# Linear attention and a gated MLP on one core: two tile transposes moved to DMA, and a 1024x1024 product made in four bursts of sixteen small products

## The chip, the core and the metric

One core of a Trainium2 chip runs the whole program as one launch. The time is device microseconds for one execution of the kernel. Comparisons are made between medians of several runs of each kernel on the same chip. One execution was also recorded by the hardware profiler; all rows below are from that execution.

## What is computed

```python
x  = A_x                                   # 1 x 2048 x 1024, bf16
xn = layernorm(x)
q, k, v = split(xn @ wqkv)                 # 32 heads of 32
pq, pk = phi(q), phi(k)                    # phi(t) = (t+1 if t>0 else exp(t)) + 1e-6
kv  = einsum("bhsd,bhse->bhde", pk, v)     # per head, 32 x 32
z   = einsum("bhsd->bhd", pk)
o   = (pq @ kv) / (pq @ z + 1e-6)
s   = o @ wo
g   = silu((silu(xn @ w_gate) * (xn @ w_up)) @ w_down)    # inner width 3584
out = x + s * g
```

The change touches two intermediate things. The first is the transposed form of xn for two of its sixteen tiles of 128 rows. The second is M, a 1024 x 1024 matrix: for each head, the transposed 32 x 32 matrix kv/z times that head's 32 rows of wo. With M, the attention half of the output is one product of the scaled pq with M.

## The kernel before, in words

**A planner writes the order.** The code first lists operations (`Plan.op`), each with an engine, the regions that it reads and writes, and an assumed cost. `Plan.schedule` then orders all engines with a list scheduler. A DMA is taken to occupy SyncE for 0.47 or 1.22 us and to land some microseconds later. Due times are counted back from the TensorE work that needs the result; for a DMA the due time moves forward by a larger allowance than for an on-chip operation. TensorE operations keep the listed order, except that within a window of six (`WINDOW=6`) the first that is ready may go ahead. The emitted program is fixed: each engine executes its list in order and waits on semaphores. One change to one operation can therefore shift the order of others. All 128-row matmul groups are recorded at line 309, all transposes on TensorE at 316, all ScalarE copies and activations at 441, all VectorE two-operand operations at 452, all plain DMA issues on SyncE at 455.

**The opening (to about 24 us).** x arrives in tiles of 128 rows. `ln_tile(i)` takes statistics on VectorE (772 to 779), a power on GpSimd (782), and normalises, on VectorE for tiles 0 and 1 and on ScalarE for the others, into one of two slots (`xn_ring`). `t_tile(i)` makes the transposed tile. For tiles 0 to `NPE-1` = 3 it uses TensorE: eight transposes of 128x128 into PSUM and a copy to SBUF; tile 2 and tile 3 each have one 128x1024 copy on ScalarE (line 821). For tiles 4 to 15 it uses one DMA transpose issued by SyncE (line 808). A slot of `xn_ring` can be filled again once its transpose has read it. Tiles 0 and 1 are multiplied by the k and v weights directly (`p_piece`, 64 matmuls of 512 columns).

**The k and v stage (to about 118 us).** Tiles 2 to 15 go in pairs u through a seven-product scheme for a 2 by 2 block product (`Set.step(m)`, m = 1 to 7, four matmuls each). Product 1 and product 2 read only the first tile of the pair; product 5 reads the sum of blocks of both tiles, made on VectorE by `x_sums(u)`. After product 1 its bank is copied on ScalarE to a second bank (`put1`), after product 5 its bank is copied to SBUF (`put5`). `a_tile(i)` adds one tile's pk^T v into three PSUM banks with eight matmuls of 129 columns. It depends only on the k and v of its own tile, and the calls stand in a queue named `fill`, from which the loop takes one after each product 6.

**M.** When kv is complete, VectorE scales and masks it and TensorE transposes it (`kvt`). `m_build(g, c)` then makes one 128 x 512 block of M from one 128x128 stationary tile (four heads on its diagonal, zeros elsewhere) and 512 columns of wo. It takes one PSUM bank, ScalarE copies the bank to a staging slot in SBUF (`mst_ring`), and SyncE stores it in DRAM. There are sixteen blocks. They are hung on steps of three column pairs of the next stage ("g 0", "u 0", "q 1") through the table `at` at lines 1696 and 1697. M is read back later by `s_load`.

**Column pairs and banks.** From `q 0` on, the work goes in pairs of sets, with a half-sized version of products 1 and 5 (`Joint`, steps nj1a to nj5d). The listed order of a pair, woven into the rest of the previous one, is

```python
LINK = "7_0 nj1a 3_0 7_1 nj1b nj5a 3_1 nj1c nj5b 4_0 nj1d nj5c 4_1 n2_0 nj5d n6_0 n2_1 n6_1".split()
```

where n marks the new pair, "6_1" is product 6 of set 1, and each plain step is four matmuls. PSUM has eight banks, dealt out in the order in which they come free in the list (`balloc`, `bfree`). A set holds two banks from product 1 on and a third, in place of the first, from product 6 on; a Joint takes two banks at its first part.

**The remainder.** The gate, up, q and s pairs and the down product follow for two halves of the rows, and take from 118 us to the end.

Of the kernel before, what the change touches and what calls it, by code (L numbers as in the profile page):

```python
# [9 lines left out]
ACT = mybir.ActivationFunctionType  # L10
# [3 lines left out]
FP16 = mybir.dt.float16  # L14
KB = 1024
# [301 lines left out]
    return last  # L317


def build_kernel(nc, A_x, A_wqkv, A_wo, B_w_gate, B_w_up, B_w_down, out, WINDOW=6, NWARM=15, NPE=4, LEAD=12.0):  # L320
    S, D, FF = 2048, 1024, 3584
    NT, KT, NG, NPAIR = 16, 8, 8, 14
    EPS_LN, EPS_PHI = 1e-5, 1e-6
# [9 lines left out]
    with ExitStack() as es:  # L333
# [20 lines left out]
        def named(*key):  # L354
            return Region([key])

        H = Arena("H", 84 * KB)
# [19 lines left out]
        m_scr = nc.dram_tensor("m_scratch", [D, D], FP16)  # L377
        m_v = m_scr.rearrange("(g p) c -> p g c", p=128)
# [13 lines left out]
        def balloc(fresh=False):  # L392

            if fresh and bare and (len(banks) < 3 or freed[bare[0]] < freed[banks[0]]):
                b = bare.popleft()
                is_bare.discard(b)
                return b
            return banks.popleft()
# [7 lines left out]
        def bfree(b):  # L406
            freed[b] = len(PL.ops)
            (bare if b in is_bare else banks).append(b)
# [7 lines left out]
        def dsem(name):  # L416
            if name not in semn:
                semn[name] = sem("d_" + name)
            return semn[name]
# [8 lines left out]
        def pe_mm(reads, writes, mms):  # L428
            return PL.op("pe", reads, writes, partial(_mm_group, mms), mm_cost(mms))
# [10 lines left out]
        def act(reads, writes, o, i, func, src="ps", **kw):  # L440
            q = PL.op("act", reads, writes, lambda h: h.activation(o, i, func, **kw),  # L441
                      nel(o) / (1000.0 if "bias" in kw or not isinstance(kw.get("scale", 1.0), float) else 1200.0)
                      + (0.055 if src == "ps" else 0.095))
            if func != ACT.Identity:
                PL.table(q, func)
            return q
# [7 lines left out]
        def dma(reads, writes, o, i, s, nbytes, cow=None, after=None):  # L454
            return PL.op("sp", reads, writes, lambda h: h.dma_start(o, i), 0.47, sem=s,  # L455
                         nbytes=nbytes * (1.45 if nbytes in (128 * KB, 896 * KB) else 1.0), cow=cow,
                         after=after)
# [114 lines left out]
        for n in range(NWARM):  # L572
            b = n % 8
# [318 lines left out]
        def a_tile(i):  # L892
            q = i % 4
            pk = pkv[i].ap()
            mms = [(kv_ap(g), pk[:, g * 128:(g + 1) * 128], vext[q][:, g, 0:129], i == 0 and g % 3 == 0, i == NT - 1)
                   for g in range(NG)]
            pe_mm([pkv[i].r, named("vx", q, 0), named("vx", q, 1), named("vx1", q), vx_r[q]], [bank_r[b] for b in kvb], mms)
# [76 lines left out]
        p_piece(1, 1, 0)  # L974
        for b in tb:
            bfree(b)
        fill = deque([partial(a_tile, 0), partial(a_tile, 1)])
        stats_of = {1: x_sums(1)}
        todo = [(u, w) for u in range(1, NT // 2) for w in range(2)]

# [19 lines left out]
        kvs(0)  # L1000
        for m in (1, 5, 2):
            sets[0].step(m)
        for n in range(len(todo)):
            cur = kvs(n)
            if todo[n][1] == 0:
                prepare(todo[n][0] + 1)
            nxt = kvs(n + 1)
            for m, k in ((6, 1), (7, 5), (3, 2), (4, 0)):
                cur.step(m)
                if nxt is not None and k:  # L1010
                    nxt.step(k)
                if k == 1 and fill:
                    fill.popleft()()
            if todo[n][1] == 1:
                while fill:
                    fill.popleft()()
                fill.extend((partial(a_tile, 2 * todo[n][0]), partial(a_tile, 2 * todo[n][0] + 1)))
# [28 lines left out]
            act([bank_r[b]], [KVT_r], KVT[:, :, :], tv[:, :, :], ACT.Identity)  # L1046
            bfree(b)

        mst_ring = Ring(H, 36 * KB, 1 * KB, 16)

        def m_build(g, c):
            b = balloc(True)
            pe_mm([KVT_r, wo_r[c]], [bank_r[b]], [(ps[b][:, :], KVT[:, g, :], wo[c][:, g, :], True, True)])
            s = mst_ring.take()
            act([bank_r[b]], [s.r], s.ap(FP16), ps[b][:, :], ACT.Identity)
            bfree(b)
            dma([s.r], [named("mscr", c)], m_scr[g * 128:(g + 1) * 128, c * 512:(c + 1) * 512], s.ap(FP16),
                dsem("mst%d" % (s.k % 4)), 128 * KB)

# [14 lines left out]
        def wload(src, joint, dt=BF16, rd=()):  # L1076


            s = raw_ring.take()
            dma(list(rd), [s.r], s.ap(dt).rearrange("p (kt n) -> p kt n", n=512), src, dsem("wr%d" % s.k), 1024 * KB)  # L1080
            v = s.ap(dt).rearrange("p (kt w n) -> p w kt n", w=2, n=256)
            c = cmb_ring.take()
            cv = c.ap(FP16).rearrange("p (m w kt n) -> p m w kt n", m=4, w=2, n=128)
            cr = [c.sub(q * 2 * KB, 2 * KB).r for q in range(4)]
            sums({(k, i): v[:, :, 4 * k:4 * k + 4, i * 128:i * 128 + 128] for k in range(2) for i in range(2)},
                 [cv[:, q] for q in range(4)], [s.r], cr)

            def block(m):
                if m in RAW_OF:
                    k, i = RAW_OF[m]  # L1090
                    return v[:, :, 4 * k:4 * k + 4, i * 128:i * 128 + 128], s.r
                return cv[:, SUM_OF[m]], cr[SUM_OF[m]]

            def stat(w, m):
                bl, r = block(m)
                return [bl[:, w, q, :] for q in range(4)], r
            inner = {}
            for m in joint:
                bl, r = block(m)
                t = in_ring.take()  # L1100
                tv = t.ap(FP16).rearrange("p (m kt n) -> p m kt n", m=4, n=128)
                tr = [t.sub(q * KB // 2, KB // 2).r for q in range(4)]
                A = {(k, i): bl[:, i, 2 * k:2 * k + 2, :] for k in range(2) for i in range(2)}
                sums(A, [tv[:, q] for q in range(4)], [r], tr)
                inner[m] = (A, r, tv, tr)

            def jstat(m, k):
                A, r, tv, tr = inner[m]
                if k in RAW_OF:
                    return [A[RAW_OF[k]][:, q, :] for q in range(2)], r  # L1110
                return [tv[:, SUM_OF[k], q, :] for q in range(2)], tr[SUM_OF[k]]
            return stat, jstat
# [175 lines left out]


        def s_load(n):  # L1290
            return wload(m_v[:, :, n * 512:(n + 1) * 512], (1, 5), FP16, [named("mscr", n)])

        st_ring = Places([(TM, o * KB) for o in (20, 24, 21, 25)], KB)

# [391 lines left out]
            last_pair[0] = q_pair(1, 0, got["q", 1, 0], {}, False)  # L1686
            return last_pair[0]

        mb = deque((g, c) for g in range(NG) for c in range(2))
        for p in range(2):  # L1690
            for k, n in order:
                st = got.pop((k, p, n))
                at = {}
                if (p, k, n) == (0, "q", 0):
                    at = {"5_1": [kv_done], "3_0": [kvt]}
                if p == 0 and (k, n) in (("g", 0), ("u", 0), ("q", 1)):
                    at = {"2_0": [build_m], "6_0": [build_m], "2_1": [build_m] * 2, "6_1": [build_m] * 2}
                if (p, k, n) == (0, "g", 1):
                    for q in range(4):
                        dma([P.reg(q * 4 * KB, 4 * KB)], [named("xscr", q)], x_scr[q], P.at(q * 4 * KB, 4 * KB, FP16),  # L1700
                            dsem("xp%d" % q), 512 * KB, after=PL.lastpe)
                if (k, n) == ("u", 1):
                    at = {"j1d": [partial(recip, p)]}
                if (k, n) == ("g", 2):
                    at = {"j1a": [partial(normalise_part, p, 0, 0)], "2_1": [partial(normalise_part, p, 0, 1)]}
                if (k, n) == ("u", 2):
                    at = {"j1a": [partial(normalise_part, p, 1, 0)], "2_1": [partial(normalise_part, p, 1, 1)], "4_1": [partial(combos, QV)]}
                if (k, n) == ("g", 3):
                    at = {"2_1": [partial(x_inner, QV, qin, QIN_AT)]}
                if last_pair[0] is not None and (p, k, n) == (1, "q", 0):  # L1710
                    pass
                elif k == "q":
                    q_pair(p, n, st, at)
                elif k == "s":
                    s_pair(p, n, st, at)
                else:
                    gu_pair(p, k, n, st, at)
                if (p, k, n) == (0, "q", 0):
                    x_inner(XV[0])
                pump(1)  # L1720
            down(p)
# [66 lines left out]
```

## Time and profile before

| what | value |
|---|---|
| median of 4 runs | 716.15 us (715.46 to 716.44) |
| profiled execution, its own time | 715.89 us |
| its span | 714.1 us |
| outside the span | 1.79 us |
| granted TensorE clock | 1.00 in every slice |
| VectorE busy | 641.5 us (90%) |
| ScalarE busy | 404.3 us (57%) |
| DMA transposes of x tiles on SyncE | 12 (four into X, eight into P) |

In the rows, PE is TensorE's matmuls and PEld its weight loads, DVE is VectorE, ACT is ScalarE, and SPq is SyncE issuing DMAs. Rows give start, duration (of a merged group, if it ends in xN) and, in brackets, idle time and what ended it. A matmul row of 512 columns shows about 380 ns for one, but matmuls are pipelined: in a long run they start every 213 ns, and that spacing is what one costs. So costs on TensorE are read from the start of one group to the start of the next.

### The profile page before, as it was taken

The page shows a single profiled execution, that of the slowest core. Times are in us where ns is not written, and L with a number is a line of the kernel's source. Part 1 is how long each engine was busy: PE and PEld are TensorE (multiplying, and loading weights), DVE is VectorE, ACT ScalarE, POOL GpSimd, SP SyncE. Part 2 cuts the span into 40 slices and gives each one's busy share as a digit, 9 for nine tenths or more (in the row PEclk, how much of TensorE's full clock was granted, in tenths as well). Part 3 has the DMA queues.
Part 4 walks back from the last instruction along what each step waited for, and adds up shares of the span by engine and source line. Part 5 has one row for each costly group of instructions (what it writes and reads, how often), then busy time and mean ns, then how long its engine had stood idle before and what let it go on. Part 6 is the DMA issues. An engine that isn't in the chain of part 4 may idle for free.

```text
span 714.1 us, 11277 instructions
## 1 busy us (share of the span) xinstructions
PE 707.1 (99%) x4149; PEld 390.5 (55%) x4149; DVE 641.5 (90%) x1533; ACT 404.3 (57%) x779; POOL 12.5 (2%) x35
## 2 busy tenths in 40 slices
PE   8999999999999999999999999999999999999997
PEld 3444445555555555556556455555555555565654
DVE  6999988989999999998957999999999999798863
ACT  3766744887679675654222157676886656621212
POOL 2011000000000000000000000000000000000000
PEclk9999999999999999999999999999999999999999
DMA  9325335136364344235595964133725241656653
GB/s 302 110 60 118 60 113 181 60 118 222 134 183 123 130 134 143 78 92 157 148 205 153 272 165 148 60 118 92 204 64 174 92 148 60 171 147 156 147 155 95
DMA packets 138758, 98.11 MB, mean 137 GB/s; under 512 B 32848, under 2 KB 135760, under 8 KB 138704
## 3 DMA queue, kind: packets, MB, share of 16 engines
q1 hardware_dynamic: 138416, 97.21, 47.9%
q8 instruction: 32, 0.52, 0.3%
q10 hardware_dynamic: 288, 0.20, 0.1%
q14 instruction: 22, 0.18, 0.1%
HBM read 77.59 MB, written 12.71 MB: 126 GB/s over the span
## 4 chain that ended last, share of the span: by engine, by line
PE 96%; ACT 2%; DMA 1%; DVE 1%; SPq 0%; issue 0%
PE ps L309 96%; DMA H<-in_A_wqkv_dram 1%; ACT TM L441 1%; ACT W L441 0%; SPq L455 0%; PE ps L316 0%; ACT ps L441 0%; DVE W L452 0%; ACT L441 0%; DVE ps L452 0%; DVE TM L452 0%; ACT X L441 0%; DVE H L851 0%; ACT H L441 0%; SPq L756 0%
## 5 line engine op out<-in xcount | busy, mean ns | idle before, releaser
L309 PE MATMUL ps<-X,W 128*128 128x512 f16 (+2 forms) x1372 | 289.2, 350 | 0.1
L441 ACT ACTIVATE TM<-ps 128x512 f16<-128x512 f32 (+3 forms) x355 | 186.8, 548 | 107.4 <-PE ps L309 104.4
L309 PE MATMUL ps<-H,W 128*128 128x512 f16 (+2 forms) x1096 | 218.9, 351 | 0.1
L452 DVE TENSOR_TENSOR W<-W 128x1024 f16<-128x1024 bf16 (+5 forms) x416 | 185.6, 480 | 6.0 <-PE ps L309 5.3
L309 PEld LDWEIGHTS ps<-X,W 128*128 128x128 f16 (+1 forms) x1372 | 132.6, 98 | 103.9 <-ACT ps L441 0.8
L309 PEld LDWEIGHTS ps<-H,W 128*128 128x128 f16 (+1 forms) x1096 | 106.0, 98 | 95.2 <-DVE ps L452 0.6
L452 DVE TENSOR_TENSOR ps<-ps,TM 128x256 f32<-128x256 f32 (+1 forms) x250 | 131.0, 526 | 12.7 <-PE ps L309 10.3
L441 ACT ACTIVATE ps<-ps 128x512 f32<-128x512 f32 (+1 forms) x174 | 85.4, 491 | 100.7 <-PE ps L309 100.3
L309 PE MATMUL ps<-P,W 128*128 128x256 f16 (+1 forms) x516 | 99.9, 319 | 0.4 <-DVE W L452 0.4
L441 ACT ACTIVATE H<-ps 128x512 f16<-128x512 f32 (+1 forms) x126 | 74.8, 604 | 41.4 <-PE ps L309 41.4
L452 DVE TENSOR_TENSOR H<-H 128x1024 f16<-128x1024 f16 (+5 forms) x126 | 71.0, 577 | 0.6 <-ACT H L441 0.4
L309 PEld LDWEIGHTS ps<-P,W 128*128 128x128 f16 (+1 forms) x516 | 50.3, 98 | 29.8 <-DVE W L452 0.7
L441 ACT ACTIVATE TM<-TM 128x512 f16<-128x512 f32 (+1 forms) x61 | 38.0, 625 | 48.3 <-DVE TM L452 48.3
L309 PE MATMUL ps<-W 128*128 128x256 f16 (+1 forms) x330 | 61.6, 282 | 0.1
L452 DVE TENSOR_TENSOR TM<-ps,TM 128x512 f32<-128x512 f32 (+3 forms) x63 | 41.6, 660 | 12.9 <-PE ps L309 12.3
L452 DVE TENSOR_TENSOR H<-H,TM 128x512 f16<-128x512 f16 x112 | 45.2, 417 | 8.4 <-ACT H L441 8.1
L309 PEld LDWEIGHTS ps<-W 128*128 128x128 f16 (+1 forms) x330 | 31.7, 98 | 31.8 <-DVE ps L452 1.9
L309 PE MATMUL ps<-H,X 128*128 128x512 bf16 (+1 forms) x150 | 35.7, 380 | 1.0 <-ACT ps L441 0.6
L309 PE MATMUL ps<-H,P 128*128 128x512 bf16 (+1 forms) x110 | 26.8, 379 | 0.0
L452 DVE TENSOR_TENSOR H<-ps,TM 128x512 f16<-128x512 f32 (+1 forms) x35 | 24.0, 685 | 2.6 <-PE ps L309 2.1
L452 DVE TENSOR_TENSOR TM<-TM,W 128x512 f16<-128x512 f16 (+1 forms) x39 | 14.1, 363 | 10.5 <-ACT TM L441 10.5
L309 PEld LDWEIGHTS ps<-H,X 128*128 128x128 f16 (+1 forms) x150 | 14.0, 98 | 17.3 <-ACT ps L441 1.1
(97 smaller groups left out, 431.9 us busy)
## 6 DMA issues: line engine op xcount, KB each, us to landing
W<-in_B_w_gate_dram SPq DMA_DIRECT2D x14, 1024.0 KB, 5.4
W<-in_B_w_up_dram SPq DMA_DIRECT2D x13, 1024.0 KB, 5.6
W<-in_B_w_down_dram SPq DMA_DIRECT2D x14, 896.0 KB, 6.2
H<-in_A_wqkv_dram SPq DMA_DIRECT2D x8, 512.0 KB, 8.2
H<-r_scratch SPq DMA_DIRECT2D x32, 128.0 KB, 3.6
W<-m_scratch SPq DMA_DIRECT2D x4, 1024.0 KB, 5.5
s_scratch<-TM SPq DMA_DIRECT2D x32, 128.0 KB, 2.4
TM<-in_A_x_dram SPq DMA_DIRECT2D x16, 256.0 KB, 3.3
```

Of the source, the lines that this page charges most:

```text
L309: last = h.matmul(o, l, r, start=st, stop=sp, skip_group_check=True)
L441: q = PL.op("act", reads, writes, lambda h: h.activation(o, i, func, **kw), nel(o) / (1000.0 if "bias" in kw or not isinstance(kw.get("sca ...
L452: return dve(reads, writes, lambda h: h.tensor_tensor(o, a, b, op), nel(o), 1.92 if fast else 0.96)
```

## The change

Four things are done. `NPE` goes from 4 to 2, so tiles 2 and 3 of x are transposed by DMA on SyncE. `a_tile(0)` and `a_tile(1)` leave the `fill` queue and are listed right after product 1 and product 5 of the first set. `m_build` now makes four blocks for one column half at once: sixteen products of 32 x 32 stationary and 512 columns, one head each, where the head's place in its group picks the PSUM bank and the group picks the 32 partitions of that bank; the planner is told 0.6 us. Four banks are copied to a 4 KB slot, and four DMAs store it, one for each group of 32 partitions. The four calls hang on "6_0" and "6_1" of the pairs "g 0" and "u 0", and nothing is left on "q 1".

```diff
-... WINDOW=6, NWARM=15, NPE=4, LEAD=12.0):
+... WINDOW=6, NWARM=15, NPE=2, LEAD=12.0):
...
-        fill = deque([partial(a_tile, 0), partial(a_tile, 1)])
+        fill = deque()
...
         for m in (1, 5, 2):
             sets[0].step(m)
+            if m != 2:
+                a_tile(m // 5)
...
-        mst_ring = Ring(H, 36 * KB, 1 * KB, 16)
-
-        def m_build(g, c):
-            b = balloc(True)
-            pe_mm([KVT_r, wo_r[c]], [bank_r[b]], [(ps[b][:, :], KVT[:, g, :], wo[c][:, g, :], True, True)])
+        mst_ring = Ring(H, 36 * KB, 4 * KB, 4)
+
+        def m_build(g0, c):
+            bb = [balloc(True) for _ in range(4)]
+            mms = []
+            for hl in range(4):
+                v = slice(32 * hl, 32 * hl + 32)
+                for k in range(4):
+                    mms.append((ps[bb[hl]][32 * k:32 * k + 32, :], KVT[v, g0 + k, v], wo[c][v, g0 + k, :], True, True))
+            pe_mm([KVT_r, wo_r[c]], [bank_r[b] for b in bb], mms).busy = 0.6
             s = mst_ring.take()
-            act([bank_r[b]], [s.r], s.ap(FP16), ps[b][:, :], ACT.Identity)
-            bfree(b)
-            dma([s.r], [named("mscr", c)], m_scr[g * 128:(g + 1) * 128, c * 512:(c + 1) * 512], s.ap(FP16),
-                dsem("mst%d" % (s.k % 4)), 128 * KB)
+            for hl, b in enumerate(bb):
+                u = s.sub(hl * KB, KB)
+                act([bank_r[b]], [u.r], u.ap(FP16), ps[b][:, :], ACT.Identity)
+                bfree(b)
+            sv = s.ap(FP16).rearrange("p (h n) -> p h n", n=512)
+            for k in range(4):
+                row = (g0 + k) * 128
+                dma([s.r], [named("mscr", c, g0, k)], m_scr[row:row + 128, c * 512:(c + 1) * 512].rearrange(
+                    "(h k) n -> k h n", h=4), sv[32 * k:32 * k + 32], dsem("mst%d_%d" % (s.k % 4, k)), 128 * KB)
...
-            return wload(m_v[:, :, n * 512:(n + 1) * 512], (1, 5), FP16, [named("mscr", n)])
+            return wload(m_v[:, :, n * 512:(n + 1) * 512], (1, 5), FP16, [named("mscr", n, g, k) for g in (0, 4) for k in range(4)])
...
-        mb = deque((g, c) for g in range(NG) for c in range(2))
+        mb = deque((g, c) for g in (0, 4) for c in range(2))
...
-                if p == 0 and (k, n) in (("g", 0), ("u", 0), ("q", 1)):
-                    at = {"2_0": [build_m], "6_0": [build_m], "2_1": [build_m] * 2, "6_1": [build_m] * 2}
+                if p == 0 and (k, n) in (("g", 0), ("u", 0)):
+                    at = {"6_0": [build_m], "6_1": [build_m]}
```

More of the change, by code (lines that the diff above doesn't have):

```diff
@@ L317, in _tr_group, with build_kernel @@
     return last
-def build_kernel(nc, A_x, A_wqkv, A_wo, B_w_gate, B_w_up, B_w_down, out, WINDOW=6, NWARM=15, NPE=4, LEAD=12.0):
+def build_kernel(nc, A_x, A_wqkv, A_wo, B_w_gate, B_w_up, B_w_down, out, WINDOW=6, NWARM=15, NPE=2, LEAD=12.0):
     S, D, FF = 2048, 1024, 3584
```

## The prediction

> **What bounds the kernel now.** I read the busy times first, then the chain that ended last, then the timeline where the change acts.
>
> ```profile
> PE 707.1 (99%) x4149; PEld 390.5 (55%) x4149; DVE 641.5 (90%) x1533; ACT 404.3 (57%) x779; POOL 12.5 (2%) x35
> ```
>
> TensorE is the bound of almost the whole span. From the answer on windows, 135 to 184 us (where M is made) has PE busy in all of its 49 us, and 18 to 24 us has PE 6.00 and DVE 6.00 of 6.00. So an edit gains what it takes from PE's issue slots, or from the few PE gaps, and loses what it adds there. The chain in order of time shows the one large gap in reach, in the opening:
>
> ```profile
> 19.18 4.33 PE ps L309 x20
> ...
> 23.53 0.47 ACT H L441
> ...
> 24.02 1.02 ACT X L441
> 25.04 0.49 ACT ps L441
> 25.53 2.27 ACT W L441 x2
> 27.80 0.97 ACT TM L441 x2
> 28.78 0.50 ACT ps L441
> ...
> 29.32 97.41 PE ps L309 x540
> ```
>
> For 5.8 us the end hangs on ScalarE's queue: the PSUM copy of tile 3's transpose (1.02), a bank copy, the normalisation of tiles 4 and 5 (2.27), then more bank copies. Only then does PE run through. The timeline of the same place:
>
> ```profile
> 18.57 0.61 PE L316 MATMUL ps<-ident,W 128*128 128x128 f16 x8
> ...
> 19.01 4.48 PE L309 MATMUL ps<-H,X 128*128 128x512 bf16 x20
> ...
> 23.33 0.61 PE L316 MATMUL ps<-ident,W 128*128 128x128 f16 x8
> ...
> 23.77 1.03 PE L309 MATMUL ps<-H,X 128*128 128x512 bf16 x4
> ...
> 29.32 1.04 PE L309 MATMUL ps<-H,X 128*128 128x512 bf16 x4 [0.59 <-ACT ps L441]
> ```
>
> Eight transposes cost from 18.57 to 19.01, and from 23.33 to 23.77: 0.44 us each time. The group before 29.32 began at 27.70 and its four matmuls fill slots to 28.56 (4 x 0.2133), so the gap is 0.76 us.
>
> **Opening: what is removed.** Two times eight transposes on PE: 2 x 0.44 = 0.88 us. Two ScalarE copies of about 1.02 us; tile 3's stands in the chain above, so bank copies behind it can come a microsecond sooner and the 0.76 us gap can close. Together at most 1.64 us. The Trainium skill's "TensorE: Matmul & The Clock Gate", Part 4, gives about 275 ns for one transpose in a kernel; sixteen would be 4.4 us. The row decides: in a run they start every 55 ns, and 0.88 us is all that PE can get back.
>
> **Opening: what is added.** Two DMA transposes, 1.33 us of SyncE each where two stand in a row (26.70, 2.70 us for two). Other such transposes of x into X:
>
> ```profile
> DMA to landing us min/median/max: 3.0/3.1/3.3
> ```
>
> Tile 2 is normalised at 17.07 to 18.31; its DMA can be issued at 18.4. The weight loads keep the queues full until about 20.2 us, so it lands near 22, and product 1 needs it at 23.77 less 0.44, 23.3, or a little less. Covered. Tile 3 is normalised at 21.64 to 22.88: landing 26.0, plus a first block sum on DVE (0.42), so product 5 can start near 26.5. The planner moves due times of what feeds a DMA forward, and ScalarE has lost one copy before it (19.21), so perhaps 25.7. Before, product 5 started at 25.97. Meanwhile PE has, from about 22.9: product 1 (0.86), a_tile 0 and 1 (0.47 each by 24.64 to 25.11), product 2 (0.86), the next set's product 1 (0.86), together 3.5 us, to 26.4. The two a_tile calls only change places: no work is added, and where the second one stood (34.51) there is no gap that it was filling. If that cover is gone, the wait on tile 3 shows at full length, up to 2 us. Behind the DMA on SyncE stand loads of later x tiles, not needed for many microseconds. The normalisation of tile 5 waits for tile 3's slot, to about 26; it ran to 27.80 before and its own transpose was issued at about 28, its product starts after 35, so a microsecond later is free. DVE has the same work; since it is full at 18 to 24 it may not follow by the whole 1.64. I take 1.2 us gained, between 1.64 gained and 1.0 lost (tile 3 late by 2 us beyond the cover, less the 0.88, rounded down).
>
> **M: TensorE.** A block of M costs one slot of 512 columns: 146.22 to the next group at 146.44. Sixteen are 16 x 0.2137 = 3.42 us. A burst does four of them. No row shows 32-row products; the nearest is the 32-column group of `recip` (all rows, four column tiles):
>
> ```profile
> 475.99 1.03 PE L309 MATMUL ps<-X,W 128*128 128x512 f16 x4
> 476.94 1.06 PE L309 MATMUL ps<-H,Zh 128*32 128x256 bf16 x32
> 477.93 0.39 PE L309 MATMUL ps<-W,TM 128*128 128x256 f16 x2
> ```
>
> The group before it fills slots to 476.85, so 0.09 us are lost going in. Its 32 products, four at a time, are eight streams of 0.1067, 0.853; the next group starts after 0.99, so 0.14 are lost coming out: 0.23 us a round trip. A burst is then 0.213 + 0.23 + the stagger of sixteen starts. Part 3 of the skill's TensorE page has starts 4 ns apart, 0.06 for fifteen: an estimate of 0.50 in all; its 660 ns for a whole pack of sixteen would gain 4 x (0.855 - 0.66) = 0.8. If starts came one by one at the 24 ns of the row's weight loads (0.78 us for 32), 16 x 0.024 = 0.39: 0.83. The row had eight weight loads active within 0.05 us, so I take 0.13, 0.57 us a burst: 4 x (0.855 - 0.57) = 1.1 us gained, between 0.1 and 1.4.
>
> **M: banks and ScalarE.** Sixteen copies remain, at the pace of
>
> ```profile
> 148.80 2.60 ACT L441 ACTIVATE H<-ps 128x512 f16<-128x512 f32 x5 [0.27 <-PE ps L309]
> ```
>
> 0.52 us each. The skill's "TensorEngine Tiling (Array Packing)" speaks against the change here, under PSUM Bottleneck: tiling speeds up TensorE, not the evacuation. At "6_0" the sets hold four banks; a burst takes the other four, waits until the last of them is copied out, and then 4 x 0.52 = 2.1 us of copies stand against 0.57 us of PE. Queued behind a burst are product 6 of set 1, whose sum takes one of these banks, then the second burst, which takes back three; and step nj1a of the next pair takes two of the second burst's (1.04 us plus about 0.3 of latency). Cover: 2_1 and 6_1 (1.7 us) after the first burst, 7_0 and 3_0 (1.7 us) after the second, within the window of six. By the rule the kernel waits each time; by the row most is covered, if the inputs of these steps are ready. ACT is busy 6.40 of 7.00 at 135 to 142 and 7.15 of 8.00 at 142 to 150 and gets eight copies per pair instead of six, 1.04 us more. I take 0.3 us lost in each pair for a first and second burst, 0.6 us in all, between 0 and the rival's 5.0. Pair "q 1" loses four copies; PE was full there, so that gives nothing more.
>
> **Edits at nothing.** Sixteen stores stay sixteen, 128 KB each, about 0.35 us of SyncE; from 32 partitions they may land later than the 2.3 us of before. M is first read back at 219 us and the last store was issued at 180.5: nearly 40 us of cover. Four stores wait together for the fourth copy, and a gate or up load queued behind them is late by at most 2 us, with the planner's lead of 12. Without the lead it would be 2 us.
>
> **Sum.** -0.88 and -0.32 in the opening (1.2), -1.1 and +0.6 in M: -1.7 us. Span 714.1 - 1.7 = 712.4, with 1.8 outside 714.2; the profiled run stands 0.26 below the median of 716.15, so the median after is 714.4 us. What is late next is again TensorE, all the way.
>
> **The rivals.** (a) *The opening gives nothing*: tile 3 or DVE, full at 18 to 24, eats all but 0.15 of it; M brings 0.5. 715.5 us. For it: DVE 6.00 of 6.00. Against: the chain goes by ScalarE, not DVE. (b) *The bursts do not overlap*: 0.83 each, M gains 0.1 and the banks take 0.6; with the opening's 1.2 gained, 715.4 (716.15 - 0.7). For it: no row has sixteen tiles. Both are within 0.2%. (c) *Slower: four banks at once.* If every burst makes PE wait out its own four copies, less one step of four matmuls (2.1 - 0.86 = 1.24), 4 x 1.24 = 5.0 us are lost, 3.9 after the 1.1; with the opening's gain +2.7, 718.8. It decides on "slower" (over 0.2%, 1.43 us, about what a measurement can tell from no change) once a burst costs over 0.93 us in waits: (1.43 + 1.1 + 1.2) / 4. For it: ACT near full there. Against: PE found other work in all of 135 to 184 us with six copies a pair.
>
> **How the numbers follow.** Forecast (both gains, small bank waits) 0.48; (a) 0.19; (b) 0.15; (c), from part to full, 0.18. A forecast case near 714.4 spreads from 713.1 (1.64 + 1.4) to 715.3, so some of it falls within 0.2% (714.7 and above, about 0.12), and (a) and (b), which stand 0.65 to 0.75 us under the median, reach "faster" with 0.10 of theirs. Of (c), 0.01 stays under 1.43 us. Faster 0.48 - 0.12 + 0.10 = 0.46, slower 0.17, same 0.37. Range 712.9 to 717.2: from all gains together to about half of (c).
>
> **What would show it.** Right: no transposes on PE after 12 us, product 5 near 26, no PE gap over 0.3 us at 24 to 31; four groups of sixteen 32x32 products, next group 0.5 to 0.65 us after each start; PE idle under 1 us at 130 to 155. Wrong: a PE wait on X or on DVE's sums near 25 (a); next group after 0.8 us or more (b); waits on ACT H around each burst (c). Also wrong if the planner's new order opens gaps elsewhere, such as near 430 us, where the chain leaves PE now.

## The result, and the profile after

The changed kernel takes 715.53 us (median of 33 runs, 713.87 to 717.09). Taken again beside it on the same chip, the kernel before took 716.44 us (53 runs, 715.23 to 717.92). The ratio of the two is 0.9987, with a 95% interval of 0.9982 to 0.9992: 0.91 us saved, between 0.57 and 1.29. That is surely not zero, but it is below the 0.2% that the prediction set as its bound for "faster".

The profiled execution of the changed kernel took 714.87 us, its span was 712.9 us, and the granted TensorE clock is full in every slice. Its busy line:

```profile
PE 704.2 (99%) x4181; PEld 388.0 (54%) x4181; DVE 640.3 (90%) x1533; ACT 403.4 (57%) x777; POOL 13.2 (2%) x35
```

TensorE is still the bound: 2.9 us less busy than before, with 32 instructions more (48 products more for M, 16 transposes fewer). ScalarE has two copies fewer. The chain that ended last shows where the path now leaves TensorE up to 140 us (start, duration, what):

```profile
10.14 1.04 PE ps L309 x4
11.18 0.45 PE ps L316 x8
11.63 106.43 PE ps L309 x584
...
132.47 1.20 DVE H L851 x2
134.01 0.44 PE ps L309 x16
134.46 15.54 PE ps L309 x112
```

The 5.8 us on ScalarE between 23.5 and 29.3 are gone: from 11.63 the chain runs through on TensorE for 106 us. What is new is the entry at 134.01, where the first burst of M (x16) hangs on VectorE by the profile's reckoning; "Where the bursts stand" tells who ended that wait.

Spans of two single executions can't be compared to a few tenths, because of how each one starts. The third group of four k products waits for its weights. Its row in the kernel before, and then in the changed kernel:

```profile
10.06 1.04 PE L309 MATMUL ps<-H,X 128*128 128x512 bf16 x4 [0.17 <-DMA H<-in_A_wqkv_dram]
```

```profile
10.14 1.04 PE L309 MATMUL ps<-H,X 128*128 128x512 bf16 x4 [0.45 <-DMA H<-in_A_wqkv_dram]
```

Over all the profiled executions of this case (one of each kernel) this start lies anywhere from 9.62 to 11.88 us, with and without the change, so it is chance. I therefore measure from this row (A) to later landmarks: the last group of `a_tile`, where the k and v stage ends; the first group of `recip` (B); and that of the second half of the rows (C). From A to the last `a_tile` the four profiles with the old opening (the kernel before, m_only, m_short_copy, no_m) agree to 0.01 us (108.69), so A is a sound start. From C to the last matmul all profiles agree to 0.01 us (233.94); from C to the end they take 237.15 to 237.20, but 237.52 in m_mid and 237.64 in m_short_copy, where the last store was issued later. The last `a_tile` before, then after:

```profile
118.75 0.63 PE L309 MATMUL ps<-H,TM 128*128 128x129 bf16 x8
```

```profile
117.42 0.63 PE L309 MATMUL ps<-H,TM 128*128 128x129 bf16 x8
```

B before, then after:

```profile
182.76 1.06 PE L309 MATMUL ps<-H,Zh 128*32 128x256 bf16 x32
```

```profile
181.16 1.06 PE L309 MATMUL ps<-H,Zh 128*32 128x256 bf16 x32
```

A to B is 172.70 us before and 171.02 after: 1.68 gained, within 0.02 of the prediction's sum. Of it, 1.41 are gained by the last `a_tile` (108.69 to 107.28) and 0.27 behind it, where M is. C starts at 476.94 before and here after:

```profile
475.73 1.06 PE L309 MATMUL ps<-H,Zh 128*32 128x256 bf16 x32
```

So B to C is 294.18 before and 294.57 after: 0.39 is given back. A to C leaves 1.29, the upper end of what the medians allow. There are three questions: what made the 1.41 in the opening, why M gave 0.27 and not the 0.5 that was forecast, and what took the 0.39.

### The profile page after: what moved, and what is told of

It reads as the page before. It is cut to its first block, busy times and chain, and to the rows that moved or that the text cites. A ratio compares the mean times of both kernels' runs of the same rounds, so it can differ in the third digit from the quotient of the medians.

```text
span 712.9 us, 11353 instructions
## 1 busy us (share of the span) xinstructions
PE 704.2 (99%) x4181; PEld 388.0 (54%) x4181; DVE 640.3 (90%) x1533; ACT 403.4 (57%) x777; POOL 13.2 (2%) x35
## 4 chain that ended last, share of the span: by engine, by line
PE 91%; DVE 5%; DMA 2%; ACT 1%; issue 0%; SPq 0%; DVEq 0%
PE ps L309 91%; DMA X<-in_A_wqkv_dram 1%; DMA H<-in_A_wqkv_dram 1%; DVE W L452 1%; DVE TM L452 1%; DVE ps L452 1%; DVE H L851 1%; DVE X L452 0%; ACT TM L441 0%; SPq L455 0%; DVE H L1037 0%; DVE P L452 0%; DVE TM L850 0%; ACT L441 0%; PE ps L316 0%
## 5 line engine op out<-in xcount | busy, mean ns | idle before, releaser
L309 PEld LDWEIGHTS ps<-H,X 128*128 128x128 f16 (+1 forms) x150 | 14.1, 98 | 17.9 <-DMA H<-in_A_wqkv_dram 1.7
L452 DVE TENSOR_TENSOR TM<-TM,W 128x512 f16<-128x512 f16 (+1 forms) x39 | 14.1, 364 | 10.5 <-ACT TM L441 10.5
```

The source lines that it names most:

```text
L309: last = h.matmul(o, l, r, start=st, stop=sp, skip_group_check=True)
L452: return dve(reads, writes, lambda h: h.tensor_tensor(o, a, b, op), nel(o), 1.92 if fast else 0.96)
```

## The experiments

**The theory** was the prediction's: the opening gives about 1.2 us from TensorE's slots and ScalarE's queue, M about 0.5, because bank waits eat half of what the bursts save. **Rivals** were: the gain is all in one of the two parts; `a_tile` in its new place is a needed cover; freed ScalarE time makes the gain in the opening; and for M, the waits follow from where the bursts stand, not from there being four banks at a time.

All runs in one table. The medians of the kernel before beside them were 716.59 (first four runs), 716.47 (next four) and 716.52 (last four). The last three columns are the differences to before in the profiled execution, from A to the last `a_tile`, to B and to C, negative for a gain. The ratio is the estimate with an interval; it need not equal the quotient of the two medians.

| run | median us | ratio, 95% interval | A to last `a_tile` | A to B | A to C |
|---|---|---|---|---|---|
| open_only | 715.69 | 0.9987 (0.9979 to 0.9995) | -1.55 | -1.55 | -0.68 |
| m_only | 716.24 | 0.9998 (0.9990 to 1.0006) | 0.01 | -0.25 | -0.28 |
| npe_only | 715.32 | 0.9982 (0.9975 to 0.9989) | -1.33 | -1.32 | -1.32 |
| m_late | 716.42 | 0.9997 (0.9988 to 1.0006) | -1.54 | -0.58 | -0.49 |
| m_two_u | 716.15 | 0.9995 (0.9985 to 1.0005) | -1.54 | (two bursts after B) | -1.16 |
| m_mid | 715.58 | 0.9982 (0.9974 to 0.9989) | -1.58 | -2.01 | -1.79 |
| act_kept | 716.15 | 0.9993 (0.9983 to 1.0003) | -1.45 | -1.71 | -0.85 |
| atile_only | 716.40 | 0.9994 (0.9985 to 1.0003) | -0.17 | -0.16 | -0.17 |
| m_short_copy | 715.08 | 0.9982 (0.9973 to 0.9991) | 0.00 | -1.41 | -1.35 |
| no_m | 713.43 | 0.9966 (0.9952 to 0.9979) | 0.00 | -3.27 | -2.98 |
| npe3 | 716.39 | 1.0000 (0.9991 to 1.0009) | -0.15 | -0.14 | -0.15 |
| npe_mid | 715.40 | 0.9988 (0.9979 to 0.9996) | -1.28 | -1.70 | -1.26 |

### The two halves apart

open_only is the kernel before with the two DMA transposes and the moved `a_tile` calls; m_only is the changed kernel with the old opening.

```diff
# open_only, against the kernel before
-... NPE=4, LEAD=12.0):
+... NPE=2, LEAD=12.0):
-        fill = deque([partial(a_tile, 0), partial(a_tile, 1)])
+        fill = deque()
+            if m != 2:
+                a_tile(m // 5)
# m_only, against the changed kernel: the same lines the other way round
```

> The opening alone: tiles 2 and 3 transposed by DMA and the two a_tile calls moved; M made as before, sixteen blocks one bank each. Theory (the opening carries the gain): span about 712.8 and median 1.3 us below before, with the recip group of the first half near 181.4 (182.76 before, 181.16 with the whole change), so that M's part is worth 0.3 us at most. Rival (the M bursts carry the gain, the opening is eaten by a full VectorE): within 0.4 us of before, recip group at 182.4 or later.

> M alone: four bursts of sixteen products at the same steps as in the changed kernel; tiles 2 and 3 transposed on TensorE, a_tile calls where they were before. Theory (bursts cost 0.46 us each, so 1.6 us come back, but a first burst waiting on four banks gives 1.2 of it away): 0.3 us below before, between 0.0 and 0.6; a TensorE gap of about 1 us before the first burst shows again. Rival (the wait of the first burst came from the shifted opening, not from the bursts): no gap at the first burst, 1.3 us or more below before.

The opening alone has the whole measured gain (0.9987, as the full change), and M alone can't be told from nothing (0.9998). Saved by the medians: 0.90 and 0.35 us (0.9 and 0.1 by the ratios); the full change saved 0.91. The profiles say which part brings what: open_only has all of its 1.55 by the last `a_tile` and nothing behind it, m_only has nothing by then and 0.25 behind it. The sum, 1.80, is within 0.12 of the full change by B. So M's part lies about halfway between nothing and the prediction's 0.5. The opening in the changed kernel, TensorE and then VectorE and SyncE from the timeline (start, duration, operation; brackets would name a wait):

```profile
23.74 1.10 PE L309 MATMUL ps<-H,TM 128*128 128x129 bf16 x16
24.68 1.89 PE L309 MATMUL ps<-H,X 128*128 128x512 bf16 x8
26.48 2.85 PE L309 MATMUL ps<-H,W 128*128 128x512 f16 x12
29.16 1.03 PE L309 MATMUL ps<-H,X 128*128 128x512 bf16 x4
...
25.40 0.68 DVE L452 TENSOR_TENSOR H<-H 128x1024 f16<-128x1024 bf16 x1
26.00 0.75 DVE L452 TENSOR_TENSOR W<-X 128x512 f16<-128x512 f16 x2
...
21.38 1.52 SPq L808 DMA_TRANSPOSE X<-W  x1
```

No bracket stands at TensorE's rows: the largest loss between two matmuls there is under 0.1 us, where before 0.76 stood ahead of 29.32. Product 5, the first reader of tile 3 (H,W), starts at 26.48. Tile 3's DMA was issued at 21.38; with some 3.1 us for such a transpose it landed near 24.5. The block sums that product 5 needs start only at 26.00, behind other VectorE work. TensorE's own work, the two `a_tile` calls and two groups of products, filled its slots to 26.40, so if anything held product 5 it was VectorE's queue, for under 0.1 us, and not the DMA.

### The opening taken apart

```diff
# npe_only: before, with this alone
-... NPE=4, LEAD=12.0):
+... NPE=2, LEAD=12.0):
# npe3: before, with NPE=3 (only tile 3 by DMA)
# atile_only: before, with only the fill queue emptied and a_tile listed after products 1 and 5
# act_kept: the changed kernel, with the two 128x1024 ScalarE copies put back, into a free place
+            if NPE <= i < 4:
+                act([s.r], [W.reg(48 * KB, 2 * KB)], W.at(48 * KB, 2 * KB, FP16), xa, ACT.Identity, "sb")
+            if i >= NPE:
                 return
```

> Tiles 2 and 3 transposed by DMA, but the two a_tile calls left in the queue that comes after product 6; M as before. Theory (a_tile covers the wait for tile 3, 0.94 us of work): TensorE stands still 0.5 to 1.0 us before product 5 at about 25.5 us, and the time is 0.5 to 1.0 us above the run with both moved, so 0.3 to 0.8 below before. Rival (tile 3 lands early enough, or the planner's window brings a_tile forward by itself): the same as with both moved, 1.3 us below before.

> The two a_tile calls moved, everything else as before. Theory (they cover nothing that was open, since the run with the DMA transposes alone lost nothing without the move): within 0.3 us of before; long run to last a_tile group 107.0 to 107.3 us. Rival (the move closes a part of the 0.76 us gap by itself): 0.5 us or more below before, 106.6 us or less. Also a further look at when the long run of k and v products starts with the tiles transposed on TensorE: 11.3 to 11.6 us in the two looks so far, 11.6 to 13.0 in the four with DMA; if that spread is chance it may be late here too.

> Before, with tile 3 alone transposed by DMA (tile 2 on TensorE), a_tile calls not moved, M as before. Theory (0.44 us for each eight transposes; the 0.76 us gap at 29 us closes with tile 3's copy gone): from the long run's start to the last a_tile group 106.0 to 106.4 us, 0.8 to 1.2 us below the 107.0 to 107.2 of before, of 1.4 to 1.8 with both tiles. Rival (the gap closes only with both): 106.6 to 106.8 us.

> The changed kernel with one copy of 128x1024 on ScalarE added for tile 2 and one for tile 3, into SBUF that nobody reads, so that ScalarE has as much to do in the opening as before. Theory (ScalarE's queue was half of the opening's gain: 0.88 us are TensorE's slots, the rest the bank copies that come sooner): from the start of the long run of k and v products to the last a_tile group 0.4 to 0.8 us more than the 105.4 to 105.8 of the runs so far with two tiles by DMA (107.2 before). Rival (all that counts is TensorE's 0.88 us, and the rest came from the planner's new order): the same length within 0.2 us.

**Moving the `a_tile` calls in the list gives nothing that the medians can tell.** Without the move the gain is about as large (0.9982, -1.32 by B), and the move alone is within the noise (0.9994, -0.16). My expectation that TensorE would stand still for 0.5 to 1.0 us was wrong, but not because no cover is needed. In npe_only the planner brought one of the two calls forward by itself, ahead of product 5:

```profile
26.55 0.63 PE L309 MATMUL ps<-H,TM 128*128 128x129 bf16 x8
27.42 2.76 PE L309 MATMUL ps<-H,W 128*128 128x512 f16 x12 [0.24 <-DVE W L452]
```

Product 5 then lost 0.4 us by slots, where the changed kernel lost under 0.1. So the cover was in part there in either case, and no run takes it away.

**The copies are no separate gain, by the profile.** With both put back, it has the same gain by B (-1.71). The medians can't show this: act_kept's can't be told from the kernel before, since its profile gives 0.86 back behind B (see "The 0.39 us given back"). The copies ran at 17.16 and 21.43, about 1.05 us each, mostly where ScalarE had been idle. The run has a limit: nobody waits for these copies, so the planner could put them into idle time, which it could not do with those of the kernel before. It shows that ScalarE's time as such is free there; it doesn't show that tile 3's copy, in its old place in the order, was.

**One tile by DMA gives nothing, which I had not expected.** From the timeline of npe3:

```profile
27.43 0.60 ACT L441 ACTIVATE TM<-ps 128x512 f16<-128x512 f32 x1
...
28.05 0.29 DVE L850 TENSOR_SCALAR TM<-TM 128x512 f16<-128x512 f16 x1 [0.87 <-ACT TM L441]
28.27 0.75 DVE L452 TENSOR_TENSOR W<-X 128x512 f16<-128x512 f16 x2
28.74 2.55 PE L309 MATMUL ps<-H,W 128*128 128x512 f16 x11 [0.88 <-DVE W L452]
```

The DMA of tile 3 was issued at 22.70, so its data were there near 26. VectorE got to the sums at 28.27 only, because ahead of them in its order stood a clamp (28.05) that waited 0.87 us for an exponential on ScalarE (27.43), itself behind the normalisation of a later tile. The 0.44 us of eight transposes were saved, and a gap of 1.04 by slots (27.23 + 0.47 for `a_tile`, to 28.74; 0.88 in the bracket) came in place of the one of 0.76: together 0.16, as measured. So the second part of the opening's gain is not "ScalarE has one copy fewer": it is that in the order which the planner finds with two tiles by DMA, no engine stands in front of product 5 for long.

### What M can give at most

no_m leaves the products and copies of M out and stores wo in its place. m_short_copy is m_only with copies of 128 of the 512 columns; the staging slot is filled from x by a DMA.

```diff
# no_m, against the kernel before
-            b = balloc(True)
-            pe_mm(...)
-            act([bank_r[b]], [s.r], s.ap(FP16), ps[b][:, :], ACT.Identity)
-            bfree(b)
-            dma([s.r], [named("mscr", c)], ...)
+            dma([KVT_r, wo_r[c]], [named("mscr", c)], ...)
# m_short_copy, against m_only
+            dma([], [s.r], s.ap(), xf[0:256, :].rearrange("(p a) c -> p (a c)", a=2), dsem("mfill%d" % s.k), 512 * KB)
-                u = s.sub(hl * KB, KB)
-                act([bank_r[b]], [u.r], u.ap(FP16), ps[b][:, :], ACT.Identity)
+                u = s.sub(hl * KB, KB // 4)
+                act([bank_r[b]], [u.r], u.ap(FP16), ps[b][:, 0:128], ACT.Identity)
```

> Before, with M's sixteen products and their sixteen copies left out; what is stored as M is wo, so the output is another. The floor of any way to make M. Theory (M's blocks cost before their slots on TensorE, 3.42 us, and nothing else, since the stretch around them lost 1.45 us only): 3.2 to 3.6 us below before. Rival (the copies on a busy ScalarE also delayed the pairs): 4 us or more below. If only 2.5 us or less come back, other waits fill the slots. A further look at the start of the long run of k and v products with TensorE transposes: 11.3 to 11.7 us if that start depends on how the tiles are transposed.

> The opening of before with M in four bursts at the steps of the changed kernel, but each ScalarE copy of an M bank moves 128 of its 512 columns (about 0.2 us instead of 0.52); three quarters of M are not copied, and what is stored there is x, loaded into the staging slot by DMA. Theory (two waits: getting four banks at the first burst, 1.24 us, and giving them back, about 0.6 us around the second bursts): the gap before the first burst stays at 1.0 to 1.4 us, the stretch from 118 to 240 us loses 0.4 to 0.8 us less than with full copies. Rival (ScalarE's total load sets the gap): the gap before the first burst falls under 0.7 us. Second rival (the copies hold nothing up): 118 to 240 us as with full copies, within 0.2 us.

Without M, 3.27 us go by B and 3.09 by the medians (2.4 by the ratio, between 1.5 and 3.4, from five runs). That is no more than the 3.42 us of sixteen slots: the kernel before paid for M with TensorE's slots alone, and all its copies were hidden. Now the price of a burst, from TensorE's timeline of the changed kernel:

```profile
147.72 0.43 PE L309 MATMUL ps<-H 32*32 32x512 bf16 x16
148.09 2.77 PE L309 MATMUL ps<-X,W 128*128 128x512 f16 x12
150.78 0.43 PE L309 MATMUL ps<-H 32*32 32x512 bf16 x16
151.38 1.36 PE L309 MATMUL ps<-X,W 128*128 128x512 f16 x7 [0.16 <-DVE ps L452]
```

All sixteen products lie within one row of 0.43 us, hardly longer than the 0.38 of a single matmul: they overlap. The next group starts 0.37 after a burst, and 0.60 after one where its bank was late. The twelve before 150.78 fill slots to 150.65 (12 x 0.2133), so 0.1 is lost going in. A burst costs 0.47, less than the 0.57 that I had taken. Four save 3.42 - 4 x 0.47 = 1.54 us of slots. m_only kept 0.25 of it by B. With short copies the gain by B is -1.41, that is nearly all of the 1.54. The planner also moved things, because it costs a short copy at less: the first burst came at 137.62 instead of 134.92. So this is not a clean subtraction, but about 1.2 us of what M loses goes with the time that four banks need to be emptied. I had expected the first burst's wait to stay at 1.0 to 1.4 us; it went.

### Where the bursts stand

```diff
# m_late, against the changed kernel
-                if p == 0 and (k, n) in (("g", 0), ("u", 0)):
+                if p == 0 and (k, n) in (("u", 0), ("q", 1)):
# m_two_u: bursts on "6_0" and "6_1" of ("u", 0) and of ("u", 1)
# m_mid: one burst on "6_1" of g 0, two on u 0, one on "6_0" of q 1
-                if p == 0 and (k, n) in (("g", 0), ("u", 0)):
-                    at = {"6_0": [build_m], "6_1": [build_m]}
+                if p == 0 and (k, n) in (("g", 0), ("u", 0), ("q", 1)):
+                    at = {"g": {"6_1": [build_m]}, "u": {"6_0": [build_m], "6_1": [build_m]}, "q": {"6_0": [build_m]}}[k]
# npe_mid: m_mid without the move of a_tile
```

> The changed kernel with the four bursts hung on the 6_0 and 6_1 steps of the pairs u 0 and q 1, not g 0 and u 0. Theory (the first burst's 1.24 us wait is the change from exponential to Silu at the start of g 0, when banks are held by the last pair's evacuations and a table load of 1.28 us): u 0 has no such change and waits under 0.4 us a burst; q 1 has one, from Silu back to Exp, and may wait there; 0.0 to 1.0 us below the changed kernel. Rival (four banks at once cost a wait wherever the first burst stands): again a TensorE gap of over 1 us before the first burst, time the same as the changed kernel within 0.3.

> The changed kernel with the four bursts hung on 6_0 and 6_1 of the pairs u 0 and u 1. Theory (a burst waits only where its four banks are still held: at g 0 by the last pair's evacuations behind a table load, at q 1 by the first burst's own four copies with one group of cover; in a pair u three groups stand between the bursts): no TensorE gap over 0.3 us at any of the four, 1.2 us below the changed kernel, 2.0 to 2.5 below before. Rival (the bursts' waits are the planner's, and come back at another place): a gap of about 1 us at u 1, or elsewhere before the next recip group, and the time of the changed kernel within 0.3.

> The changed kernel with one burst on 6_1 of g 0, two on 6_0 and 6_1 of u 0, one on 6_0 of q 1. Theory: the burst on 6_1 of g 0 comes after the held banks are free, the one on q 1 has no burst before it: no gap over 0.4 us, about 1.0 us below the changed kernel, as with both bursts in pairs u. Rival (whatever burst is the first in g 0 waits 1.2 us): a gap of about 1.2 us at the first burst, time of the changed kernel within 0.3.

> The two parts that did best: tiles 2 and 3 by DMA without moving the a_tile calls, and M's bursts on 6_1 of g 0, 6_0 and 6_1 of u 0 and 6_0 of q 1. Theory (parts add up): 1.5 to 1.9 us below before, about 0.6 below the changed kernel. Rival (what one part brings is waited away later, at the load of the second half's q weights near 386 us): 1.2 us or less below before, with a gap near 410 us.

First the wait that the chain showed at 134.01, in the timeline of the changed kernel, with what ScalarE and VectorE do ahead of it:

```profile
131.54 1.28 ACT L441 ACT_TABLE_LOAD   x1
...
132.40 1.27 DVE L851 SCALAR_TENSOR_TENSOR H<-ps,TM 128x512 bf16<-128x512 f32 x2
132.83 1.08 ACT L441 ACTIVATE TM<-ps 128x512 f16<-128x512 f32 x2
...
134.01 0.44 PE L309 MATMUL ps<-H 32*32 32x512 bf16 x16 [1.24 <-DVE TM L452]
```

The burst needs four free banks at once. By the order in which kernel.py deals out banks, one of the four had long been free; one was the last of `q 0`, read by VectorE (851) to 133.67; and two belonged to the new pair `g 0` itself: the bank of its first Silu and that of its product 5, which ScalarE empties from 132.83 to 133.91. The bracket names VectorE, but the instruction that it names, `TM<-W` at 133.59, works from SBUF to SBUF and reads no bank; TensorE's own wait for ScalarE's semaphore ended at 133.96, so ScalarE came last. Both ScalarE copies stood behind the table load for the Silu at 131.54. Yet the load isn't what makes the wait. It can explain only about a quarter of a microsecond (an estimate: VectorE's bank came free at 133.67, 0.24 before ScalarE's, and that read didn't wait for the load). And m_late, m_two_u and no_m, which have no work of M at this place, have the same load even earlier (13.5 us after the last `a_tile`, against 14.1 here) and no loss over 0.3 us around it. What is new is a burst that asks for these banks as soon as it is listed. The same wait is in m_only and act_kept. A plain block of the kernel before needed one bank, and found it.

m_late moves the bursts away from there. On u 0 both run without such a wait, as in the changed kernel. On q 1 the second burst meets rival (c). Its timeline:

```profile
161.47 0.43 PE L309 MATMUL ps<-H 32*32 32x512 bf16 x16
161.83 1.04 PE L309 MATMUL ps<-X,W 128*128 128x512 f16 x4
162.01 2.06 ACT L441 ACTIVATE H<-ps 128x512 f16<-128x512 f32 x4 [1.14 <-PE ps L309]
...
164.13 0.44 PE L309 MATMUL ps<-H 32*32 32x512 bf16 x16 [1.26 <-ACT H L441]
```

One group of four matmuls stands between the bursts, the four copies of the first burst end at 164.07, and TensorE waits 1.26 us: rival (c)'s arithmetic, 2.1 - 0.86 = 1.24. On u 0 three groups (12 x 0.2133 = 2.56 us) stand between, more than the 2.06 of the copies, and there is no wait. So the long waits are a matter of place: either some of the four banks are still held by other work, or a second burst follows closer than its predecessor's copies. They aren't all: behind the last `a_tile` m_late is 0.96 us slower than the kernel before, while the changed kernel, with a wait as long, is 0.27 faster. The rest is in smaller waits.

m_two_u has no wait over 0.3 us at any burst, and yet gains no more by C (-1.16) than the changed kernel (-1.29); I had expected 1.2 us more. Summed over all matmuls, with a burst as one slot, what TensorE loses beyond its slots grows from 0.83 in the changed kernel to 1.97 us at 183 to 240, of which 0.5 is the ordinary cost of the two bursts that stand there, and from 1.77 to 2.35 at 240 to 350: several waits of 0.2 to 0.4 us in place of one long one. m_mid takes the first burst past the end of q 0. Of the kernels that still make all of M it keeps the most by B (-2.01, 0.33 more than the changed kernel), but waits of 0.51 for VectorE at 132.90 (open_only, without any burst, has 0.31 at the same place) and 0.34 lost at 165.03 take part of it back, so the theory that the long wait would simply vanish was half right. npe_mid is put together from the two best parts. By B they add, within 0.06 us: -1.28 by the last `a_tile` (npe_only -1.33), and -0.42 behind it (m_mid -0.43). By C 0.44 is gone again in a gap at 409.56, so -1.26 is left. That is close to what the rival in its expectation had said (1.2 or less, with a gap near 410), and the median (0.9988) is no better than that of either part. npe_only, m_mid and m_short_copy have the lowest ratios of those that keep a product M (0.9982), but their intervals overlap that of the full change, and I don't claim a better kernel.

### The 0.39 us given back

B to C is 294.16 to 294.28 in m_only, npe_only, m_late, atile_only, m_short_copy and npe3 and in the kernel before, 294.47 in no_m, and 294.40 to 295.05 in m_mid, after, npe_mid, act_kept and open_only. In the changed kernel:

```profile
408.29 1.03 PE L309 MATMUL ps<-W 128*128 128x512 f16 x4
409.56 0.39 PE L309 MATMUL ps<-W 128*128 128x256 f16 x2 [0.24 <-DVE ps L452]
```

Four matmuls fill 0.85, so 0.41 is lost ahead of 409.56; in act_kept and open_only it is 0.87 and 0.86. VectorE, which it waits for, was itself held up at 394.22:

```profile
394.22 0.69 DVE L452 TENSOR_TENSOR X<-X 128x1024 f16<-128x1024 bf16 x1 [0.48 <-DMA X<-in_A_wqkv_dram]
```

This transfer was issued at 386.02 (8.17 us to landing), 1.1 us earlier than before (387.14), while TensorE was 1.6 us earlier. The missing half microsecond is in two DMA transposes ahead of it on SyncE, before and then after:

```profile
382.39 2.50 SPq L1592 DMA_TRANSPOSE TM<-TM  x2
```

```profile
380.76 3.01 SPq L1604 DMA_TRANSPOSE TM<-TM  x2
```

The first of the two held SyncE for 1.70 us instead of 1.20, and VectorE waited 0.48. In act_kept it took 2.17, VectorE waited 0.94 and TensorE lost 0.87. Over the fourteen profiles this transpose took 1.55 to 2.17 us in the changed kernel, act_kept, m_two_u, m_mid and npe_mid, and each of these loses 0.2 us or more near 410; it took 1.36 in m_late and 1.20 in the others, and of those only open_only has the gap, with a load that took longer to land (9.15 us). So the 0.39 is a late load. With one profile of each kernel, whether an order makes the transpose long or chance does can't be told. no_m is the earliest of all and has no such gap, so "TensorE is earlier" doesn't settle it, and no run was made for this wait alone.

## Why the prediction came out as it did

**The bound and the place of the gain: right.** TensorE is the bound before and after, the transposes and the gap near 29 are gone, and by B the profile gains what the sum said. That it meets the sum so closely is luck: the opening brought 0.2 more than forecast and M 0.2 less. The median saved 0.91 where 1.75 was forecast (716.15 to 714.4), and so fell among the outcomes within 0.2%, which the prediction had given 0.37, and not in "faster", which it had given 0.46.

**The opening (-1.2): right in direction, somewhat small.** By the last `a_tile` it gave -1.41 in the changed kernel, -1.55 in open_only, -1.33 in npe_only. The -0.88 of sixteen transposes at 55 ns each is what the rows said. The remainder was taken at -0.32 and the 0.76 us gap closed nearly whole. The time of product 5 was forecast near 26 to 26.5 and is 26.48, but for another reason: tile 3 was normalised 1.5 us sooner than before (20.12, not 21.64) and landed near 24.5, not at 26.0, so TensorE's own work and VectorE's queue set it. That the two `a_tile` calls had to be moved was wrong: in npe_only the planner brought one forward itself. How much cover tile 3 needs was not tested. That the closed gap came from one copy fewer on ScalarE is not shown, and npe3 speaks against it.

**The bursts (-1.1): too small a gain.** They cost 0.47 each, not 0.57: -1.54. The stagger of sixteen starts that I added (0.13) is hardly there; the 0.23 for going in and out was right. Rival (b), 0.83 each, is refuted by the rows.

**The bank waits (+0.6): this is the term that failed.** I spread 0.3 us over each pair and said that TensorE idles under 1 us at 130 to 155. The runs show about 1.3 us lost against before (of the 1.54, 0.27 is left): a single wait of 1.24 at the first burst, and some 0.2 at a second burst (0.60 instead of 0.37), less small waits of before that are gone. I looked for the wait between a burst and the work listed behind it, and for u 0 judged that well. I took four banks to be free when the first burst came ("a burst takes the other four"). One was: the others were held by the last read of q 0 and by g 0's own first Silu and product 5. Rival (c)'s mechanism is real (m_late, 1.26 us), but it decides only where a second burst comes after one group. Both errors on M together left -0.27 in the changed kernel and -0.25 in m_only instead of -0.5.

**The edits at nothing: right.** The sixteen stores land 2.4 us after issue (2.3 before), and no wait on them or on M's read-back appears.

**Gaps elsewhere: right that they may come.** 0.39 us went at 410, to a load of weights that came late. It was not in the sum, and it alone brings the -1.68 of A to B down to the -1.29 of A to C. The medians have 0.91, with the 1.29 at the edge of the interval. What the last 0.4 is can't be told from single profiles, where the landing of the first weights alone moves the end by 2 us.

## What to carry to other kernels

Where the bound engine is full, concurrent small products are worth their slots only if their banks are free when they come and are emptied before the next burst: list which work holds each bank at that point, not only what is queued behind. A step that waits for k banks at once waits for the last of k evacuations; count the matmuls between two such steps against the time of the copies (here 12 covered 2.06 us and 4 did not). And when a planner writes the order, test each part alone, and look at the order that it found: leaving out an edit isn't leaving out its effect if the planner then makes the move itself. Landmarks in the profile separate parts that medians can't: here the parts add up within 0.12 us by B, while the medians are uncertain by 0.4 us or more and also carry a late load.

## What the runs showed of the hardware

Sixteen 32x32 products of 512 columns ran in 0.43 us by the row and took 0.47 us of a full stream, with 0.1 of it going in: four slots' work in about two. The third group of k products, which waits for its weights, started between 9.62 and 11.88 us over the fourteen profiled executions, although SyncE issued the same transfers in the same order. Whether this makes most of the spread of some 3 us between runs of one kernel (713.87 to 717.09) is not shown, with one profile of each. A DMA transpose that held SyncE for 1.20 us in eight of the profiles held it for 1.36 to 2.17 in the other six, and in the changed kernel and act_kept, at 1.70 and 2.17, VectorE waited 0.48 and 0.94 for a transfer behind it.
